# Scores of a decay attention: q and k taken as float32 products of 64 rows per head, in place of float16 halves turned by DMA

## The chip, the cores and the metric

The kernel runs on one core of a Trainium2 chip. A core has a matrix engine (TensorE: PE for its products, PEld for its weight loads), a vector engine (VectorE: DVE), a scalar engine (ScalarE: ACT), GpSimd (POOL) and SyncE (SP), which here only issues transfers. The metric is the device time of one execution in microseconds; lower is better.

## The reference

Decay attention over 8 batches of 8 heads (576 tokens, 64 numbers per head), then a two-layer block over the 4608 tokens:

```python
scores = scale * np.matmul(q, k.transpose(0, 1, 3, 2))
cum = np.cumsum(np.log(np.clip(f, 0.0001, 1.0)), axis=-1)
decay = cum[:, :, :, None] - cum[:, :, None, :]
scores = np.where(causal, -1e9, scores + decay)
attn = softmax(scores)               # rows
x = np.matmul(attn, v)               # to (4608, 512)
h = x @ w_in                         # 512 x 2048
g = np.where(h >= 1, h, np.where(h <= -1, 0, (h + 1) ** 2 / 4))
out = g @ w_out                      # 2048 x 512
```

## The kernel before

**Units of work.** Attention goes by pairs of heads. `jobs` lists 36 pairs p: batch 0 is cut in two by rows (8 jobs, p = 0 to 7), batch 1 gives p = 8 to 11, batches 2 to 7 give p = 12 to 35, four to a batch. A pair's scores are made in row blocks r = 0 to 4 of 128 rows (the last has 64, and holds both heads in the two halves of the partitions), each over the columns up to its diagonal: 128, 256, 384, 512 and 576 wide.

**How q and k are made ready** (`prepare`, lines 385 to 427; `early_prepare`, lines 362 to 383). For p under NQK = 12 the two heads lie side by side in the 128 partitions after PE has turned the blocks (line 377) and ACT has copied them out of PSUM (lines 381 and 383). The copy of q goes to two places, one per head, where the other head's 64 partitions are zero; so a head's score is one float32 product over 128 rows (line 481). From p = 12 on, q and k are scaled and split into float16 halves: ACT takes the largest size (line 395), `across` spreads it over the partitions with two small PE products (lines 120 and 130) and some DVE steps, `scale_of` makes the scales, ACT writes the high parts (lines 413 and 414), DVE the low parts and a copy (lines 415, 418, 422), and one DMA transpose on SP's queue turns all of it into `qkT` (line 425). A head's score is then two float16 products over 128 rows, high and low parts stacked (line 487).

**What follows a score block.** POOL builds the decay row (lines 491 and 495), DVE adds it to the product and takes the minimum (line 574), ACT makes the exponentials (line 578), ACT and DVE write float16 halves (lines 592 and 598), a DMA transpose turns them (lines 604 and 607), and PE multiplies by v (line 618). Of the accumulators, tile `s` has two buffers of 512 columns, one for each head of a block; tile `big` has one buffer of 1024 columns, which takes both heads of block r = 4 and the products with v.

**The two-layer block** runs in units of 256 tokens by 256 of the 2048 columns: 24 products at line 660 (48 shorter ones where the tokens straddle two batches) and 12 at line 688, with ACT and DVE between them (lines 669 to 674). The last loop of the function spreads the units that are ready over the four pairs of a batch, so some 18 units of the batch before lie between the steps of a batch's pairs, and the last units run alone at the end.

**Order.** The tile framework orders each engine's instructions by a simulated timeline of its own; each engine then runs its list in that order.

Of the kernel before, what the change touches and what calls it, by code (L numbers as in the profile page):

```python
# [8 lines left out]
F32 = mybir.dt.float32  # L9
F16 = mybir.dt.float16  # L10
# [19 lines left out]
NQK = 12  # L30
# [16 lines left out]
def kernel(  # L47
# [18 lines left out]

    nc = tc.nc
# [15 lines left out]
    ncut = NPAIR * sum(len(c) for c in CUTS.values())  # L83
# [55 lines left out]
    cq = const.tile([P, NT5, B * H], F32, name="cq")  # L139

    def decay_sums():
# [22 lines left out]
        nc.vector.tensor_copy(cq.rearrange("p t n -> p (t n)"), pt[:, 0:NT5 * nb])  # L164
# [138 lines left out]
    for t in qk32 + [v32]:  # L303
        nc.gpsimd.memset(t, 0.0)
# [6 lines left out]
    def load(ji):  # L311
# [9 lines left out]
        for j, src in enumerate((q, k)):  # L321
            s_ = src[w.b, h0:h0 + 2]
            t0 = 0 if j else w.r0
            nt = w.r1 - t0
            x = flat[:, j * 2 * NT5 * D:j * 2 * NT5 * D + 2 * nt * D]
            w.x32.append(x)
            if ji < NQK:
                dst = x.rearrange("p (t h d) -> p h t d", t=nt, h=2)
            else:
                dst = x.rearrange("p (h t d) -> p h t d", t=nt, h=2)  # L330
                if ji < max(NQK, ncut) + 2 and w.r1 == NT5:
                    nc.gpsimd.memset(dst[64:P, :, nt - 1, :], 0.0)
# [22 lines left out]
    early_qk = [two.tile([P, 3, 2, SP], F16, name="qkT") for i in range(2)]  # L355
    early_qk = [t.rearrange("p c h s -> p (c h s)").bitcast(F32)[:, 0:3 * S].rearrange("p (c s) -> p c s", c=3) for t in early_qk]
    cq8 = const.tile([P, NT5, 2 * H], F32, name="cq8")
    for t in early_qk:
        for h in range(2):
            nc.gpsimd.memset(t[64 - 64 * h:128 - 64 * h, h, :], 0.0)  # L360

    def early_prepare(w):

        if w.p == 0:
            nc.vector.tensor_scalar(out=cq8, in0=cq[:, :, 0:2 * H], scalar1=8.0, scalar2=None, op0=ALU.mult)
        t_ = early_qk[(w.p + NQK) % 2]
        w.nsig, w.nalpha = -8.0, -0.125
        bh = w.b * H + 2 * w.hp
        w.cqs = cq8[:, :, bh:bh + 2]
        w.q, w.k = t_, t_[:, 2]  # L370
        for j in range(2):
# [6 lines left out]
            if j == 0:  # L378
                for h in range(2):
                    rows = slice(64 * h, 64 * h + 64)  # L380
                    nc.scalar.activation(t_[rows, h, 0:n], pt[rows, 0:n], AF.Copy)
            else:
                nc.scalar.activation(t_[:, 2, 0:n], pt[:, 0:n], AF.Copy)

    def prepare(w):
        if w.p < NQK:
            return early_prepare(w)
        p = w.p
        bh = w.b * H + 2 * w.hp
        nq, nk = w.r1 - w.r0, w.r1  # L390
        qs = one.tile([P, 3, 2, NT5, P], F16, name="qs").rearrange("p c h t e -> p (c h t e)")
        m2 = tiny.tile([P, 2], F32, name="m2q")
        for j in range(2):
            n = w.x32[j].shape[1]
            nc.scalar.activation(qs[:, j * 2 * NT5 * D:j * 2 * NT5 * D + n], w.x32[j], AF.Abs, accum_out=m2[:, j:j + 1])  # L395
        mk = tiny.tile([P, 2], F32, name="mk")
        across(mk, m2)
        sc = tiny.tile([P, 2], F32, name="sc")
        scale_of(sc, mk, mk)
        sig = tiny.tile([P, 1], F32, name="sig")  # L400
        nc.vector.tensor_scalar(out=sig, in0=sc[:, 0:1], scalar1=sc[:, 1:2], scalar2=8.0, op0=ALU.mult, op1=ALU.mult)
        w.nsig = tiny.tile([P, 1], F32, name="nsig")
        nc.vector.tensor_scalar(out=w.nsig, in0=sig, scalar1=-1.0, scalar2=None, op0=ALU.mult)
        w.nalpha = tiny.tile([P, 1], F32, name="nalpha")
        nc.vector.reciprocal(w.nalpha, w.nsig)
        w.cqs = tiny.tile([P, NT5, 2], F32, name="cqs")
        nc.vector.tensor_scalar(out=w.cqs, in0=cq[:, :, bh:bh + 2], scalar1=sig, scalar2=None, op0=ALU.mult)

        nqe = 2 * nq * P
        qq = qs[:, 0:nqe].rearrange("p (b e) -> p b e", e=P)  # L410
        kk = qs[:, nqe:nqe + 4 * nk * P].rearrange("p (c b e) -> p c b e", c=2, e=P)
        xq, xk = (x.rearrange("p (b d) -> p b d", d=D) for x in w.x32)
        nc.scalar.activation(qq[:, :, 0:D], xq, AF.Copy, scale=sc[:, 0:1])
        nc.scalar.activation(kk[:, 0, :, 0:D], xk, AF.Copy, scale=sc[:, 1:2])
        nc.vector.scalar_tensor_tensor(
            out=qq[:, :, D:P], in0=xq, scalar=sc[:, 0:1], in1=qq[:, :, 0:D], op0=ALU.mult, op1=ALU.subtract
        )
        nc.vector.scalar_tensor_tensor(
            out=kk[:, 1, :, 0:D], in0=xk, scalar=sc[:, 1:2], in1=kk[:, 0, :, 0:D], op0=ALU.mult, op1=ALU.subtract
        )  # L420
        dup = kk.rearrange("p c b e -> p (c b) e")
        nc.vector.tensor_copy(dup[:, :, D:P], dup[:, :, 0:D])
        n = nqe + 4 * nk * P
        qkT = two.tile([P, 3, 2, SP], F16, name="qkT").rearrange("p c h s -> p (c h s)")
        nc.sync.dma_start_transpose(qkT[:, 0:n].rearrange("p (b e) -> p b e", e=P), qs[:, 0:n])
        w.q = qkT[:, 0:nqe].rearrange("p (h s) -> p h s", h=2)
        w.k = qkT[:, nqe:n].rearrange("p (c h s) -> p c h s", c=2, h=2)
# [33 lines left out]
    def scores(w, r):  # L461

        wid = min(P * (r + 1), S)
        q0 = P * r
        sds = []
        for h in range(2):
            p0, p1 = (0, P) if r < LAST else (64 * h, 64 * h + 64)
# [10 lines left out]
            for c0 in range(0, wid, 512):  # L478
                c1 = min(wid, c0 + 512)
                if w.p < NQK:  # L480
                    nc.tensor.matmul(  # L481
                        sp[p0:p1, c0:c1], lhsT=w.q[:, h, q0 - w.s0:q0 - w.s0 + p1 - p0], rhs=w.k[:, c0:c1],
                        start=True, stop=True,
                    )
                    continue
                for c in range(2):
                    nc.tensor.matmul(  # L487
                        sp[p0:p1, c0:c1], lhsT=w.q[:, h, q0 - w.s0:q0 - w.s0 + p1 - p0],
                        rhs=w.k[:, c, h, c0:c1], start=(c == 0), stop=(c == 1),
                    )  # L490
            nc.gpsimd.tensor_scalar(  # L491
                out=sd[p0:p1, 0:wid], in0=w.ck[h][p0:p1, 0:wid], scalar1=w.nsig if w.p < NQK else w.nsig[p0:p1],
# [67 lines left out]
    def weights(w, r):  # L560
# [11 lines left out]
        for i, (sd, sp) in enumerate(sds):  # L572
            a = sd[:, 0:wid]
            nc.vector.tensor_tensor_reduce(  # L574
                out=a, in0=sp[:, 0:wid], in1=a, scale=w.nalpha, scalar=BIG, op0=ALU.add, op1=ALU.min,
# [269 lines left out]
```

## Time and profile before

| | |
|---|---|
| median of 3 runs | 1206.32 us (1205.17 to 1208.73) |
| the profiled execution | 1203.55 us, of which 1201.8 us is the span of the profile |
| busy share: PE, DVE, ACT, POOL | 88%, 69%, 66%, 37% |
| products on PE | 8577 |
| share of 16 DMA engines | 62% |
| mean granted clock of PE | 0.95 |

A busy share is a mean over the whole span; its first 300 us (batches 0 and 1, and the weights' conversion), the 750 us after (batches 2 to 7) and the last 150 us (the two-layer block alone) differ, and the prediction reads them apart. In a row of the timeline the first number is the start, the second how long the row's merged instructions took from the first start to the last end; products on PE overlap each other, so the step from one row's start to the next row's start says what a row occupied.

### The profile page before, as it was taken

Reading aid. Unit: us, or ns where it says so; the run is one execution under the profiler, and the core shown is the slowest. Engines: PE = TensorE matmul, PEld = TensorE weight load, DVE = VectorE, ACT = ScalarE, POOL = GpSimd, SP = SyncE. Lnnn points to the kernel's source line nnn. Section 1 sums busy time; section 2 is a strip of 40 time slices with the busy share of each in tenths; the row PEclk is TensorE's granted clock in tenths of the full one; section 3 lists DMA queues with packets and bytes.
Section 4 is the critical chain, followed back from the end, with each engine's and each line's share of the span. In section 5 each row is a group of like instructions: output and inputs, shape, how many; then the busy total and the mean of one; then the engine's idle time right before and its main releaser. Section 6 shows DMA issues by size and latency. Waiting matters only on the chain. (4 is left out here: it accounts for less than half of the span.)

```text
span 1201.8 us, 24489 instructions
## 1 busy us (share of the span) xinstructions
PE 1063.1 (88%) x8577; PEld 696.6 (58%) x8577; DVE 834.0 (69%) x2399; ACT 796.6 (66%) x1666; POOL 450.5 (37%) x699
## 2 busy tenths in 40 slices
PE   4577678997699979998999999998899889999998
PEld 3444344564466656666666666656665566677665
DVE  6879989885777687769666868757776778522222
ACT  4675665974677687858677668857776767644443
POOL 5648634642544254425342325423542354000000
PEclk9878788998699999999999999999999989999999
DMA  8857544778887678677755848776978586300000
GB/s 239 254 174 189 130 122 97 137 142 181 160 144 158 146 164 153 147 161 158 145 121 127 155 88 173 153 148 134 169 141 180 115 155 113 73 19 2 18 19 18
DMA packets 439259, 160.05 MB, mean 133 GB/s; under 512 B 414944, under 2 KB 415968, under 8 KB 439136
## 3 DMA queue, kind: packets, MB, share of 16 engines
q1 hardware_dynamic: 439136, 158.49, 62.3%
q8 instruction: 67, 1.10, 0.4%
q14 instruction: 56, 0.46, 0.1%
HBM read 75.64 MB, written 9.58 MB: 71 GB/s over the span
## 5 line engine op out<-in xcount | busy, mean ns | idle before, releaser
L660 PE MATMUL ph<-x,place 128*128 128x256 f16 (+3 forms) x4608 | 451.2, 251 | 23.3 <-DVE u L671 15.5
L688 PE MATMUL po<-place,g 128*128 128x512 f16 x1728 | 426.3, 384 | 18.8 <-ACT g L673 12.5
L660 PEld LDWEIGHTS <-place 128*128 128x128 f16 x4608 | 368.3, 100 | 108.1 <-issue 29.4
L688 PEld LDWEIGHTS <-g 128*128 128x128 f16 x1728 | 163.8, 99 | 184.1 <-ACT g L673 17.0
L491 POOL TENSOR_SCALAR sdr<-ck,nsig,cqs 128x128 f32<-128x128 f32 (+1 forms) x192 | 163.6, 856 | 176.4 <-DVE pr L598 160.5
L578 ACT ACTIVATE sdr<-sdr,nm 128x384 f32<-128x384 f32 (+1 forms) x248 | 138.1, 557 | 73.2 <-DVE nm L574 65.8
L671 DVE SCALAR_TENSOR_TENSOR u<-ph,z,u 128x512 f32<-128x512 f32 x136 | 101.4, 746 | 108.2 <-ACT u L670 107.1
L669 ACT ACTIVATE u<-ph,z 128x512 f32<-128x512 f32 x136 | 104.5, 768 | 91.2 <-PE ph L660 91.0
L491 POOL TENSOR_SCALAR sd<-ck,nsig,cqs 64x576 f32<-64x576 f32 x48 | 46.6, 971 | 276.7 <-DMA ck<-cum_d 85.1
L673 ACT ACTIVATE g<-u,z 128x512 f16<-128x512 f32 x136 | 97.5, 718 | 78.9 <-DVE u L671 78.4
L674 DVE SCALAR_TENSOR_TENSOR g<-u,z,g 128x512 f16<-128x512 f32 x136 | 103.9, 765 | 62.1 <-ACT g L673 61.6
L598 DVE SCALAR_TENSOR_TENSOR pr<-sdr,rc,pr 128x384 f16<-128x384 f32 (+2 forms) x232 | 125.5, 570 | 27.1 <-ACT pr L592 26.3
L592 ACT ACTIVATE pr<-sdr,rc 128x384 f16<-128x384 f32 (+1 forms) x236 | 119.7, 555 | 18.0 <-issue 6.3
L574 DVE CUSTOM_DVE_ANT_0 sdr<-s,sdr,nalpha 128x128 f32<-128x128 f32 (+1 forms) x192 | 103.8, 544 | 23.0 <-POOL sdr L495 10.6
L495 POOL TENSOR_SCALAR_AFFINE_SELECT sdr<-sdr 128x128 f32<-128x128 f32 x248 | 97.3, 403 | 10.5
L487 PE MATMUL s<-qkT 128*128 128x128 f16 (+3 forms) x384 | 85.0, 310 | 17.9 <-DVE nm L574 17.3
L670 ACT ACTIVATE u<-u 128x512 f32<-128x512 f32 x144 | 89.8, 623 | 2.5
L487 PEld LDWEIGHTS <-qkT 128*128 128x128 f16 (+1 forms) x576 | 46.6, 103 | 58.1 <-issue 35.0
L618 PE MATMUL big<-pT,vs 128*64 128x320 f16 (+3 forms) x1098 | 72.4, 284 | 2.0 <-DVE nm L574 2.0
L395 ACT ACTIVATE qs<-qk 128x640 f16<-128x640 f32 x48 | 34.9, 729 | 52.8 <-DMA qkT<-qs 44.9
L618 PEld LDWEIGHTS <-vs 128*64 128x64 f16 x1098 | 49.4, 112 | 30.2 <-issue 8.0
L481 PE MATMUL s<-qkT 128*128 128x128 f32 (+3 forms) x128 | 53.5, 520 | 10.6 <-DVE nm L574 8.8
(169 smaller groups left out, 1170.8 us busy)
## 6 DMA issues: line engine op xcount, KB each, us to landing
ck<-cum_d SPq DMA_DIRECT2D x64, 288.0 KB, 3.8
out_dram<-ot SPq DMA_DIRECT2D x36, 256.0 KB, 2.5
qk<-in_k_dram SPq DMA_DIRECT2D x64, 128.0 KB, 2.9
ck<-in_v_dram SPq DMA_DIRECT2D x28, 288.0 KB, 3.1
v<-in_v_dram SPq DMA_DIRECT2D x62, 128.0 KB, 2.8
qk<-in_q_dram SPq DMA_DIRECT2D x56, 128.0 KB, 2.6
place<-in_moe_w_in_dram SPq DMA_DIRECT2D x12, 512.0 KB, 5.4
place<-in_moe_w_out_dram SPq DMA_DIRECT2D x10, 512.0 KB, 6.6
```

What stands on the lines that cost most here:

```text
L487: nc.tensor.matmul(sp[p0:p1, c0:c1], lhsT=w.q[:, h, q0 - w.s0:q0 - w.s0 + p1 - p0], rhs=w.k[:, c, h, c0:c1], start=(c == 0), stop=(c == 1),)
L491: nc.gpsimd.tensor_scalar(out=sd[p0:p1, 0:wid], in0=w.ck[h][p0:p1, 0:wid], scalar1=w.nsig if w.p < NQK else w.nsig[p0:p1], scalar2=w.cqs[p ...
L574: nc.vector.tensor_tensor_reduce(out=a, in0=sp[:, 0:wid], in1=a, scale=w.nalpha, scalar=BIG, op0=ALU.add, op1=ALU.min, accum_out=nm[:, i:i ...
L578: nc.scalar.activation(a, a, AF.Exp, bias=nm[:, i:i + 1], scale=-1.0, accum_out=sm[:, i:i + 1])
L592: nc.scalar.activation(pr[:, :, 0, i, :], a, AF.Copy, scale=rc[:, i:i + 1])
L598: nc.vector.scalar_tensor_tensor(out=pr[:, :, 1, i, :], in0=a, scalar=rc[:, i:i + 1], in1=pr[:, :, 0, i, :], op0=ALU.mult, op1=ALU.subtract,)
L618: nc.tensor.matmul(av[64 * h:64 * h + 64, at + s0:at + s1], lhsT=w.vs[:, vl, h, t, :], rhs=w.pT[:, t, pl, h, s0:s1], start=(t == 0 and pi ...
L660: nc.tensor.matmul(ph[:, fi, a0:a1], lhsT=wi[fb][:, wl, t, fi * P:(fi + 1) * P], rhs=xs[b][:, t, xl, s0:s0 + a1 - a0], start=(fi == 0 and ...
L669: nc.scalar.activation(u, h, AF.Relu, scale=z.u[:, i:i + 1], bias=z.h[:, i:i + 1])
L671: nc.vector.scalar_tensor_tensor(out=u, in0=h, scalar=z.t[:, i:i + 1], in1=u, op0=ALU.max, op1=ALU.min)
L674: nc.vector.scalar_tensor_tensor(out=g[:, 1], in0=u, scalar=z.r[:, i:i + 1], in1=g[:, 0], op0=ALU.mult, op1=ALU.subtract)
L688: nc.tensor.matmul(po[ch][i], lhsT=g[:, gl, fi * TC + i * P:fi * TC + (i + 1) * P], rhs=wo[fb][:, wl, fi, :], start=(first and fi == 0 and ...
```

## The change

`prepare` becomes one function for all 36 pairs: PE turns q and k blocks in float32 (line 362 after the change), ACT copies q once and k once, the two heads lying in partitions 0 to 63 and 64 to 127. A head's score is one float32 product over its own 64 partitions (line 417); the zeros beside q are gone, and so are, for p from 12 on, the largest sizes, scales, halves and the DMA transpose. The scales become the constants -8 and -0.125. In a score block the products of the two heads are written next to each other in the program.

```diff
     def prepare(w):
-        if w.p < NQK:
-            return early_prepare(w)
...
-            nc.scalar.activation(qs[:, j * 2 * NT5 * D:j * 2 * NT5 * D + n], w.x32[j], AF.Abs, accum_out=m2[:, j:j + 1])
-        across(mk, m2)
-        scale_of(sc, mk, mk)
...
-        nc.scalar.activation(qq[:, :, 0:D], xq, AF.Copy, scale=sc[:, 0:1])
-        nc.scalar.activation(kk[:, 0, :, 0:D], xk, AF.Copy, scale=sc[:, 1:2])
-        nc.vector.scalar_tensor_tensor(
-            out=qq[:, :, D:P], in0=xq, scalar=sc[:, 0:1], in1=qq[:, :, 0:D], op0=ALU.mult, op1=ALU.subtract
-        )
...
-        nc.vector.tensor_copy(dup[:, :, D:P], dup[:, :, 0:D])
-        nc.sync.dma_start_transpose(qkT[:, 0:n].rearrange("p (b e) -> p b e", e=P), qs[:, 0:n])
+        t_ = two.tile([P, 2, S], F32, name="qkT")
+        w.cqs = cq8[:, :, bh:bh + 2]
+        w.q, w.k = t_[:, 0], t_[:, 1]
+        for j in range(2):
+            pt = ps1.tile([P, 1024], F32, name="big")
+            t0 = 0 if j else w.r0
+            n = w.s1 - P * t0
+            for c0 in range(0, n, P):
+                m = min(P, n - c0)
+                nc.tensor.transpose(pt[:, c0:c0 + m], w.x32[j][0:m, c0:c0 + P], ident[0:m, 0:m])
+            nc.scalar.activation(t_[:, j, 0:n], pt[:, 0:n], AF.Copy)
...
     def scores(w, r):
-                for c in range(2):
-                    nc.tensor.matmul(
-                        sp[p0:p1, c0:c1], lhsT=w.q[:, h, q0 - w.s0:q0 - w.s0 + p1 - p0],
-                        rhs=w.k[:, c, h, c0:c1], start=(c == 0), stop=(c == 1),
-                    )
+        for c0 in range(0, wid, 512):
+            c1 = min(wid, c0 + 512)
+            for h, (p0, p1) in enumerate(rows):
+                nc.tensor.matmul(
+                    sds[h % len(sds)][1][p0:p1, c0:c1],
+                    lhsT=w.q[64 * h:64 * h + 64, q0 - w.s0:q0 - w.s0 + p1 - p0],
+                    rhs=w.k[64 * h:64 * h + 64, c0:c1], start=True, stop=True,
+                )
```

PE's list before, at a score block 256 columns wide of a pair past 12: the two float16 products of one head, a product of the two-layer block, then those of the other head.

```order
L487 LDWEIGHTS qkT
L487 MATMUL s<-qkT 128x256
L487 LDWEIGHTS qkT
L487 MATMUL s<-qkT 128x256
L688 LDWEIGHTS g
L688 MATMUL po_9811<-place_97,g 128x512
L487 LDWEIGHTS qkT
L487 MATMUL s<-qkT 128x256
L487 LDWEIGHTS qkT
L487 MATMUL s<-qkT 128x256
```

PE's list after, at blocks r = 3 (`s`, 512 wide) and r = 4 (`big`, 64 rows per head) of such a pair; L417 is a float32 product of 64 rows, L621 and L593 are the two-layer block's.

```order
L417 MATMUL big<-qkT 64x512 x2
L417 MATMUL s<-qkT 128x512
L621 LDWEIGHTS g
L621 MATMUL po_11910<-place_91,g 128x512
L621 LDWEIGHTS g
L621 MATMUL po_11910<-place_91,g 128x512
L621 LDWEIGHTS g
L621 MATMUL po_11911<-place_91,g 128x512
L621 LDWEIGHTS g
L621 MATMUL po_11911<-place_91,g 128x512
L417 MATMUL s<-qkT 128x512
L417 MATMUL big<-qkT 64x64 x2
```

A head has one product where it had two; the two heads of block r = 3 stand apart here, with products of 128 rows between them, while those of block r = 4 stand together. Over the 24 pairs from p = 12 on, the list after has 192 such products for r = 0 to 3, in 142 separate places; 41 times the two heads of a block stand side by side (15 of 128 columns, 13 of 256, 8 of 384, 5 of 512).

PE's list after, where a pair's q is turned (L362) ahead of the first score block of the pair before it:

```order
L362 MATMUL big<-ident,qk_1_115 128x128 x4
L362 MATMUL big<-ident,qk_1_115 128x64
L417 MATMUL s<-qkT 128x128 x2
L621 LDWEIGHTS g
L621 MATMUL po_10998<-place_95,g 128x512
```

These five turns, and five more for k, were not on PE for p from 12 on. Two stretches of SP's list, before and after, where a pair's q and k are fetched (qk), its decay row (ck) and the values:

```order
L607 DMA_TRANSPOSE pT<-pr_6372 128x10x64 x2
L442 DMA v_116<-in_v_dram 128x4x64 x2
L444 DMA v_116<-in_v_dram 64x2x64
L708 DMA out_dram<-ot 128x512 x2
L335 DMA qk_0_114<-in_q_dram 128x4x64 x2
L339 DMA qk_0_114<-in_q_dram 64x2x64
L425 DMA_TRANSPOSE qkT<-qs 128x30x128
L346 DMA ck<-cum_d 128x576
```

```order
L540 DMA_TRANSPOSE pT<-pr_6130 128x10x64 x2
L378 DMA v_116<-in_v_dram 128x4x64 x2
L380 DMA v_116<-in_v_dram 64x2x64
L330 DMA qk_0_114<-in_q_dram 128x4x64 x2
L334 DMA qk_0_114<-in_q_dram 64x2x64
L330 DMA qk_0_114<-in_k_dram 128x4x64 x2
L334 DMA qk_0_114<-in_k_dram 64x2x64
L641 DMA out_dram<-ot 128x512 x2
L341 DMA ck<-cum_d 128x576
```

The transpose of 30 blocks is gone from SP's list; the fetches around it stay.

More of the change, by code (lines that the diff above doesn't have):

```diff
@@ L29 @@
 NPE = 5
-NQK = 12
 POOL_LOW = {6: (2, 4), 7: (2, 4)}
@@ L163, in decay_sums @@
             )
-        nc.vector.tensor_copy(cq.rearrange("p t n -> p (t n)"), pt[:, 0:NT5 * nb])
+        nc.vector.tensor_scalar(
+            out=cq8.rearrange("p t n -> p (t n)"), in0=pt[:, 0:NT5 * nb], scalar1=8.0, scalar2=None, op0=ALU.mult
+        )
     place = [const.tile([P, 2, 2 * DM], F16, name=f"place{i}") for i in range(2 * NB + 1)]
@@ L302 @@
     sd4 = [const.tile([P, SP], F32, name=f"sd4_{i}") for i in range(2)]
-    for t in qk32 + [v32]:
-        nc.gpsimd.memset(t, 0.0)
+    nc.gpsimd.memset(v32, 0.0)
     for t in sd4:
@@ L326, in load @@
             w.x32.append(x)
[L327 to L332, printed above, removed]
+            dst = x.rearrange("p (t h d) -> p h t d", t=nt, h=2)
             full = min(w.r1, LAST)
@@ L354, with prepare @@
     prs = [one.tile([P, PRN[r]], F16, name=f"pr{r}").bitcast(F32) for r in range(NT5)]
[L355 to L367, printed above, removed]
+    def prepare(w):
+        t_ = two.tile([P, 2, S], F32, name="qkT")
         bh = w.b * H + 2 * w.hp
         w.cqs = cq8[:, :, bh:bh + 2]
-        w.q, w.k = t_, t_[:, 2]
+        w.q, w.k = t_[:, 0], t_[:, 1]
         for j in range(2):
@@ L477, in scores @@
                 sds.append((sd, sp))
[L478 to L485, printed above, removed]
-                for c in range(2):
-                    nc.tensor.matmul(
-                        sp[p0:p1, c0:c1], lhsT=w.q[:, h, q0 - w.s0:q0 - w.s0 + p1 - p0],
-                        rhs=w.k[:, c, h, c0:c1], start=(c == 0), stop=(c == 1),
-                    )
+        for c0 in range(0, wid, 512):
[5 more added lines that the diff above has]
+                    rhs=w.k[64 * h:64 * h + 64, c0:c1], start=True, stop=True,
+                )
+        for h, (p0, p1) in enumerate(rows):
+            sd = sds[h % len(sds)][0]
             nc.gpsimd.tensor_scalar(
-                out=sd[p0:p1, 0:wid], in0=w.ck[h][p0:p1, 0:wid], scalar1=w.nsig if w.p < NQK else w.nsig[p0:p1],
+                out=sd[p0:p1, 0:wid], in0=w.ck[h][p0:p1, 0:wid], scalar1=-8.0,
                 scalar2=w.cqs[p0:p1, r, h:h + 1], op0=ALU.mult, op1=ALU.add,
```

42 lines of the change are left out of this document (3 added, 39 removed).

## The prediction

> **What bounds the kernel now.** I read the busy time by stage first, then the chain of waits, then PE's timeline where it is dense. By stage (columns: stretch, its length, then busy us of PE, PEld, DVE, ACT, POOL with instruction counts, granted clock, DMA share, GB/s):
>
> ```profile
> 0.00:300.00 300.00, 221.69 (x1316) 135.44 (x1317) 241.55 (x745) 190.49 (x425) 158.51 (x232) 0.88 0.67 167
> 300.00:1050.00 750.00, 693.99 (x6049) 460.33 (x6049) 549.83 (x1601) 542.49 (x1151) 291.97 (x468) 0.97 0.73 144
> 1050.00:1201.00 151.00, 147.46 (x1214) 100.79 (x1212) 42.60 (x57) 63.64 (x91) 0.00 (x0) 1.00 0.04 15
> ```
>
> In the first 300 us PE idles 78 us and DVE is the busiest (242). In the 750 us that hold the pairs from p = 12 on, PE is busy 694 and idle 56, DVE and ACT near 73%: PE is the bound. Is a busy PE a full PE? The chain of waits, where the two-layer block runs alone:
>
> ```profile
> 1077.13 2.59 PE po L688 x12
> 1079.72 2.68 PE ph L660 x48
> ```
>
> Twelve products of 512 columns in 2.59 us are 216 ns each, one column per 0.42 ns, without a pause. The middle stage shows the same step (0.43 for two such products, from 874.32 to 874.75 below), so its PE has 56 us to give and no more. Its waits are few (columns: who waited for whom, us, times, longest):
>
> ```profile
> PE s L487 <- DVE nm L574: 16.7, 14, 5.2
> PE ph L660 <- DVE u L671: 12.9, 7, 3.4
> PE po L688 <- ACT g L673: 8.8, 7, 2.8
> ...
> PEld L487 <- issue: 33.3, 58, 5.6
> ```
>
> The last row is the weight load from `qkT`; "issue" means the profile shows nothing that it waited for, and the DMA transpose that writes `qkT` is what is left.
>
> **What leaves PE, per pair from p = 12.** A row's price is the step to the next row's start. PE's timeline at such a pair:
>
> ```profile
> 860.70 0.27 PE L120 MATMUL s<-ident,m2q 128*2 128x128 f32 x1
> 860.81 0.28 PE L487 MATMUL s<-qkT 128*128 128x128 f16 x2
> 860.92 1.84 PE L660 MATMUL ph<-x,place 128*128 128x64 f16 x30
> ...
> 866.04 0.38 PE L130 MATMUL s<-dg,ones 2*128 2x2 f32 x2
> 866.35 0.93 PE L660 MATMUL ph<-x,place 128*128 128x192 f16 x13
> ...
> 868.84 0.38 PE L487 MATMUL s<-qkT 128*128 128x256 f16 x2
> 869.06 0.59 PE L688 MATMUL po<-place,g 128*128 128x512 f16 x2
> ...
> 872.26 0.49 PE L487 MATMUL s<-qkT 128*128 128x384 f16 x2
> 872.58 1.06 PE L660 MATMUL ph<-x,place 128*128 128x64 f16 x16
> 873.57 0.69 PE L487 MATMUL big<-qkT 128*64 128x512 f16 x8
> 874.19 0.29 PE L660 MATMUL ph<-x,place 128*128 128x64 f16 x2
> 874.32 0.59 PE L487 MATMUL s<-qkT 128*128 128x512 f16 x2
> 874.75 0.28 PE L660 MATMUL ph<-x,place 128*128 128x64 f16 x2
> ```
>
> One head takes 0.11, 0.22, 0.32 and 0.43 us for its blocks r = 0 to 3 (two products each): 1.08, two heads 2.16. Block r = 4 takes 0.62, line 130 takes 0.31, line 120 takes 0.11, and two entries into a smaller shape take some 0.09 each (shown below). That is 3.38 us; times 24 pairs, **81 us leave PE**.
>
> **What comes to PE.** The pairs under p = 12 have float32 products already, and turned q and k:
>
> ```profile
> 41.51 0.86 PE L377 MATMUL big<-ident,qk 128*128 128x128 f32 x5
> 42.29 0.27 PE L120 MATMUL s<-ident,m 128*1 128x128 f32 x1
> ...
> 263.75 0.60 PE L660 MATMUL ph<-x,place 128*128 128x256 f16 x4
> 264.27 1.20 PE L481 MATMUL big<-qkT 128*64 128x512 f32 x8
> 265.41 0.72 PE L660 MATMUL ph<-x,place 128*128 128x256 f16 x5
> 265.96 0.81 PE L481 MATMUL s<-qkT 128*128 128x384 f32 x2
> 266.61 0.93 PE L660 MATMUL ph<-x,place 128*128 128x256 f16 x7
> 267.38 1.02 PE L481 MATMUL s<-qkT 128*128 128x512 f32 x2
> 268.24 0.71 PE L660 MATMUL ph<-x,place 128*128 128x256 f16 x5
> ```
>
> - *Products, r = 0 to 3.* A float32 product (two records, x2) of 384 columns takes 0.65, of 512 columns 0.86: twice the float16 pair. I give 64 rows the price of 128, as it is the columns that stream. By columns a head costs 0.22 + 0.43 + 0.65 + 0.86 = 2.16, two heads 4.3, 24 pairs 104 us.
> - *Heads that overlap.* Where both heads stand side by side, do they run at once? For halves of the output columns they do: block r = 4 in float32 has two heads of 576 columns, alone 0.97 each (0.86 x 576 / 512), and took 1.14 with entry and exit. For halves of the rows no row of this trace shows it; the ends are nothing and a whole head saved. By the count in the order (15 of 128, 13 of 256, 8 of 384, 5 of 512) that is 15 x 0.22 + 13 x 0.43 + 8 x 0.65 + 5 x 0.86 = 18 us. I take 18, by the nearest row, the one of block r = 4.
> - *Block r = 4.* 1.14 by the row above, 24 times 27; eleven of the 24 stand in pieces in the order, so 30.
> - *Entering and leaving the row halves.* From 263.75 four products of 0.109 end at 264.18, and the next starts at 264.27: 0.09 to enter. Five turns from 41.51 take 0.78; four full ones at a quarter of a 512-column record (0.107) and one half make 0.48, so entering and leaving the 64-row shape took 0.30. The 142 places are then 24 us (0.17, what block r = 4 paid: 1.14 less 0.97) to 43; I take 0.25, 36 us.
> - *Turning q and k.* 2 x 0.78 a pair, 37 us; a few share their entry with a product beside them, so 35.
>
> Together 104 - 18 + 30 + 36 + 35 = 187, less 81: **PE gains 106 us of work** in a stage in which it idles 56.
>
> The Trainium skill ("TensorE: Matmul & The Clock Gate", Part 3) says that products in different row groups run at once, some 4 ns apart; by it the 18 us are saved, without it the sum is 124. The Trainium skill ("TensorEngine Tiling (Array Packing)", Gotcha 1: PSUM Pressure) says that different row tiles cannot use one bank of PSUM at the same time. Both heads of block r = 4 write one buffer of `big`; by that page they would run one after the other, and the sum would be 19 us higher (24 x 0.8).
>
> **What leaves the other engines.** The rows (mean ns of one before the bar's end):
>
> ```profile
> L395 ACT ACTIVATE qs<-qk 128x640 f16<-128x640 f32 x48 | 34.9, 729 | 52.8 <-DMA qkT<-qs 44.9 <-issue 6.8 <-DMA qk<-in_q_dram 1.1
> L413 ACT ACTIVATE qs<-qk,sc 128x640 f16<-128x640 f32 x24 | 19.7, 820 | 3.3 <-DVE sc L110 3.1
> L383 ACT ACTIVATE qkT<-big 128x576 f32<-128x576 f32 x8 | 5.2, 645 | 2.0 <-PE big L377 1.9
> L415 DVE SCALAR_TENSOR_TENSOR qs<-qk,sc,qs 128x640 f16<-128x640 f32 x24 | 23.7, 987 | 2.9 <-ACT qs L413 2.6
> L425 SPq DMA_TRANSPOSE qkT<-qs x24: 4500/4730/5660, 269.6 to 998.3; - x24
> ```
>
> Per pair ACT loses two passes of 0.73 and two of 0.82 (line 414 like 413) and gains two copies of 0.645: 1.8 us less. DVE loses two splits of about 1.0 and more small steps, over 2 us; SP's queue loses a transpose of 4.7 us. None of these is the bound, so this pays only through PE's 56 us of waiting. Gone with certainty is the wait on the transpose; waits on DVE and ACT shrink, since both do less while PE takes longer over a pair. Ends: nothing and 56 us back; I take 30. What is late next: the copies out of `big`, in the rivals. In the first 300 us the lone float32 heads pay the same visits, some 15 us of PE against 78 of idle, and one ACT copy a pair goes; DVE's weight conversion, untouched, leads there. I count 0, ends -10 and +15.
>
> **Sum.** 106 - 30 = 76 us more than the profiled execution's 1203.55, which lies 2.8 under the median of 1206.32: 1280 against 1204, or **1282** against the median.
>
> **The rivals.**
> - *The row halves do not overlap.* Then 18 us come back, and with block r = 4 one after the other 19 more: 1319. For it: no row shows row halves at work. Against: the column halves overlap in float16 and float32.
> - *`big` becomes the wait.* It has one buffer, and per pair two more uses, each held until ACT has copied. The turns of the early pairs waited:
>
> ```profile
> L377 PE MATMUL big<-ident,qk 128*128 128x128 f32 x72 | 15.8, 339 | 15.0 <-issue 3.9 <-DVE x L628 3.5 <-ACT qkT L381 3.4
> ```
>
>   15 us over 12 jobs, 1.25 a job, 24 pairs: +30, so 1312. Against: the order puts products of the two-layer block between most turns and what needs them.
> - *Faster: the added work falls into PE's gaps.* If entering and leaving cost nothing between two products (-36), the added work is 70 us, 2.9 a pair. If all 56 us of waiting go, and the granted clock of the middle stage rises from 0.97 to 1 (0.03 x 694 = 21), that makes 70 - 77 = -7: 1199. It decides where the added work falls under 3.2 us a pair (77 / 24); I count 4.4. Against it stand the 0.09 and the 0.30, read in this trace.
>
> **How the numbers follow.** Forecast 0.62, no overlap 0.18, `big` 0.13, gaps 0.07. What this kernel's measurement can tell from no change is about 0.3%, 4 us. The gaps' case splits into 0.05 faster and 0.02 the same; the rest is slower, 0.93. The low end keeps most of the 56 us as given back and visits at 0.17 (1282 - 26 - 11 = 1245, and 5 for the early stage); the high end takes in both other slower cases (1319, 1312) and an idle time that gives back little. Range 1240 to 1340.
>
> **What would show it.** In the profile after: PE busy in the middle stage above 95% and the tail as before; lone products of line 417 at 0.43 us per record of 512 columns, and where heads stand side by side, a step of some 0.9 us for two heads (1.7 would mean no overlap); gaps of 0.1 to 0.2 us on both sides of a lone head; ACT and DVE less busy; no wait on a transpose of q and k. The forecast is wrong if 64-row products stream faster than 128-row ones, or if PE's idle time in the middle stage does not shrink.

## The result and the profile after

The changed kernel took **1238.31 us** (median of 4 runs, 1237.71 to 1241.65) against 1205.81 for the kernel before (4 runs): ratio **1.027**, 95% interval 1.0245 to 1.0295. It is slower, as forecast, but by 32.5 us where 76 were forecast; 1238 lies 2 us under the low end of the range. The profiled execution took 1237.71, of which 1235.7 is the span. One run of the kernel before, among those measured later, took 2146.17 us; no ratio below counts it.

First the busy time by stage of the profile after, with the columns as before:

```profile
0.00:300.00 300.00, 238.40 (x1332) 134.32 (x1332) 237.08 (x736) 183.31 (x413) 154.25 (x222) 0.86 0.66 162
300.00:1050.00 750.00, 743.42 (x5970) 454.66 (x5971) 453.11 (x1229) 499.29 (x1016) 224.43 (x459) 0.99 0.53 111
1050.00:1235.00 185.00, 181.05 (x1445) 120.55 (x1443) 59.98 (x98) 83.91 (x131) 3.82 (x8) 1.00 0.10 25
```

In the middle stage PE idles 7 us of 750 where it idled 56. DVE fell by 97 us, ACT by 43, POOL by 68, the DMA share from 0.73 to 0.53, and the granted clock rose from 0.97 to 0.99. The stage after 1050 us is longer by 34: what PE did not get done among the pairs is done at the end. PE's waits between 300 and 1085 us show the same thing; the three that led before (16.7, 12.9 and 8.8 us) are now:

```profile
PE s L417 <- DVE nm L507: 3.8, 4, 2.0
PE ph L593 <- DVE u L604: 1.4, 1, 1.4
...
PE po L621 <- ACT g L606: 0.4, 1, 0.4
```

PE's timeline after shows what a product of half the rows occupies (start, duration, shapes; a price is the step to the next start):

```profile
701.80 0.91 PE L417 MATMUL s<-qkT 64*128 64x384 f32 x2
702.64 0.72 PE L593 MATMUL ph<-x,place 128*128 128x256 f16 x5
...
707.17 1.12 PE L417 MATMUL s<-qkT 64*128 64x512 f32 x2
708.23 1.90 PE L621 MATMUL po<-place,g 128*128 128x512 f16 x8
...
714.70 1.18 PE L417 MATMUL big<-qkT 64*64 64x512 f32 x6
715.82 1.90 PE L621 MATMUL po<-place,g 128*128 128x512 f16 x8
...
739.48 0.80 PE L362 MATMUL big<-ident,qk 128*128 128x128 f32 x5
740.02 0.75 PE L417 MATMUL s<-qkT 64*128 64x256 f32 x4
...
744.38 0.92 PE L417 MATMUL s<-qkT 64*128 64x384 f32 x4
745.22 2.03 PE L593 MATMUL ph<-x,place 128*128 128x256 f16 x17
```

One head of 384 columns alone takes 0.84 us (701.80 to 702.64). Two of them side by side take 0.84 as well (744.38 to 745.22, x4). A lone head of 512 columns takes 1.06, where its two records stream for 0.86.

Because busy times have modelled ends, I also counted PE's time from the starts of consecutive products, from 300 us to the end: a product's columns at 0.417 ns (0.834 in float32) is streaming; extra steps at a change to or from a smaller shape are "shape"; the extra step between the two records of a 64-row float32 product is "load" (about 0.1 us); the few ns between any two products are "small"; the excess while the granted clock is under 1 is "clock"; the rest is "wait". The count begins with the first product that starts after 300 us, so a wait across that moment is left out: 8.1 us in e10_passes_again, 4.0 in e11_all_again, 3.9 in e1_full_rows, 2.0 in the changed kernel, 1.0 or less in the others. The sorting is mine and good to some us (all in us):

| kernel | streaming | shape | load | small | clock | wait | total |
|---|---|---|---|---|---|---|---|
| before | 773.3 | 21.7 | 0 | 18.3 | 14.6 | 69.6 | 897.5 |
| after | 837.3 | 43.3 | 13.9 | 18.7 | 6.3 | 10.4 | 929.8 |
| e1_full_rows | 850.7 | 24.6 | 0 | 20.2 | 4.1 | 16.9 | 916.5 |
| e2_one_s_tile | 815.4 | 38.9 | 9.5 | 18.2 | 4.2 | 33.7 | 919.8 |
| e3_twice_before | 850.0 | 24.3 | 0 | 20.4 | 3.7 | 28.3 | 926.6 |
| e5_late_one_tile | 806.8 | 36.9 | 9.3 | 19.1 | 4.3 | 28.7 | 905.1 |
| e7_twice_after | 942.0 | 40.3 | 13.1 | 21.0 | 4.9 | 11.8 | 1033.1 |
| e8_early_halves | 775.3 | 21.7 | 0 | 18.7 | 15.2 | 73.3 | 904.2 |
| e9_transposes_again | 843.6 | 45.8 | 16.4 | 19.8 | 4.9 | 29.7 | 960.1 |
| e10_passes_again | 835.1 | 42.5 | 13.4 | 18.7 | 4.2 | 8.5 | 922.4 |
| e11_all_again | 836.8 | 43.7 | 13.5 | 18.8 | 8.3 | 18.9 | 940.1 |
| e12_late_one_full_turns | 806.8 | 31.9 | 11.2 | 17.6 | 8.3 | 22.5 | 898.4 |

So PE gained 64.0 + 21.6 + 13.9 = **99.5 us of work** (forecast: 106), and got back 59.2 of waits and 8.3 of slow clock, **67.5 us** (forecast: 30). The difference, 32, is the result. The first 300 us bring no difference: by their end PE has started 614 products into `ph` and `po` in either kernel. The open question is why so much came back.

The row of weight loads at the lone head of 512 columns tells where "load" arises:

```profile
707.17 0.29 PEld L417 LDWEIGHTS s<-qkT 64*128 64x128 f32 x2 [0.42 <-issue]
```

Both loads have ended by 707.46, and the second record starts at 707.70: it does not wait for its own weights. What is late is the first record's load, which starts only as that record does; the step to the second record is 0.53 there. The 128-row float32 products of e1_full_rows show the same rule at 512 columns: where the first record's load begins 0.11 us or more ahead of it the step is 0.43, at 0.08 ahead it is 0.46, at 0.05 it is 0.49, and 0.53 where it begins with the record.

### The profile page after: what moved, and what is told of

Same layout as the page of the kernel before. It is cut to its first block, busy times and chain, and to the rows that moved or that the text cites. A ratio compares the mean times of both kernels' runs of the same rounds, so it can differ in the third digit from the quotient of the medians.

```text
span 1235.7 us, 24329 instructions
## 1 busy us (share of the span) xinstructions
PE 1162.9 (94%) x8745; PEld 709.5 (57%) x8745; DVE 750.2 (61%) x2062; ACT 766.5 (62%) x1558; POOL 382.5 (31%) x689
## 5 line engine op out<-in xcount | busy, mean ns | idle before, releaser
L593 PE MATMUL ph<-x,place 128*128 128x256 f16 (+3 forms) x4608 | 437.3, 249 | 7.8 <-POOL place L226 3.9
L593 PEld LDWEIGHTS <-place 128*128 128x128 f16 x4608 | 353.8, 99 | 115.8 <-issue 54.0
L621 PE MATMUL po<-place,g 128*128 128x512 f16 x1728 | 415.7, 382 | 4.1 <-ACT g L606 3.4
L424 POOL TENSOR_SCALAR sdr<-ck,cq 128x384 f32<-128x384 f32 (+1 forms) x248 | 162.4, 655 | 465.1 <-DVE pr L531 398.5
L621 PEld LDWEIGHTS <-g 128*128 128x128 f16 x1728 | 162.4, 98 | 188.7 <-issue 18.2
L417 PE MATMUL s<-qkT 64*128 64x512 f32 (+3 forms) x512 | 181.0, 520 | 11.2 <-DVE nm L507 9.6
L602 ACT ACTIVATE u<-ph,z 128x512 f32<-128x512 f32 x136 | 104.7, 770 | 115.2 <-PE ph L593 114.6
L507 DVE CUSTOM_DVE_ANT_0 sdr<-s,sdr 128x384 f32<-128x384 f32 (+1 forms) x248 | 119.5, 491 | 70.4 <-PE s L417 53.0
L417 PEld LDWEIGHTS s<-qkT 64*128 64x128 f32 x512 | 66.4, 204 | 62.3 <-DVE nm L507 23.2
L424 POOL TENSOR_SCALAR sd<-ck,cq 64x576 f32<-64x576 f32 x64 | 52.0, 813 | 152.3 <-DMA ck<-cum_d 104.5
L428 POOL TENSOR_SCALAR_AFFINE_SELECT sdr<-sdr 128x128 f32<-128x128 f32 x248 | 89.7, 372 | 13.4
L362 PE MATMUL big<-ident,qk 128*128 128x128 f32 (+1 forms) x328 | 61.3, 295 | 11.7 <-DVE x L561 3.5
L363 ACT ACTIVATE qkT<-big 128x576 f32<-128x576 f32 (+2 forms) x72 | 43.5, 604 | 32.4 <-PE big L362 31.5
```

The source lines that it names most:

```text
L417: nc.tensor.matmul(sds[h % len(sds)][1][p0:p1, c0:c1], lhsT=w.q[64 * h:64 * h + 64, q0 - w.s0:q0 - w.s0 + p1 - p0], rhs=w.k[64 * h:64 * h ...
L424: nc.gpsimd.tensor_scalar(out=sd[p0:p1, 0:wid], in0=w.ck[h][p0:p1, 0:wid], scalar1=-8.0, scalar2=w.cqs[p0:p1, r, h:h + 1], op0=ALU.mult, o ...
L507: nc.vector.tensor_tensor_reduce(out=a, in0=sp[:, 0:wid], in1=a, scale=-0.125, scalar=BIG, op0=ALU.add, op1=ALU.min, accum_out=nm[:, i:i + 1],
L593: nc.tensor.matmul(ph[:, fi, a0:a1], lhsT=wi[fb][:, wl, t, fi * P:(fi + 1) * P], rhs=xs[b][:, t, xl, s0:s0 + a1 - a0], start=(fi == 0 and ...
L602: nc.scalar.activation(u, h, AF.Relu, scale=z.u[:, i:i + 1], bias=z.h[:, i:i + 1])
L621: nc.tensor.matmul(po[ch][i], lhsT=g[:, gl, fi * TC + i * P:fi * TC + (i + 1) * P], rhs=wo[fb][:, wl, fi, :], start=(first and fi == 0 and ...
```

## The experiments

Three theories. **Length**: PE waits less because its own list got longer, so that the steps of DVE and ACT that it waits for are done in time; then work added to PE alone gives the waits back too. **Relief**: PE waits less because DVE and ACT lost the passes over q and k; then putting those back brings the waits back. **Transfers**: it is the lost DMA transposes. A second set of runs asks for the price of the row halves. The kernel before was measured beside each set of runs, at 1205.81 to 1209.30 us, so a difference of 3 us or so between runs of different sets says nothing.

### Only more work on PE

The kernel before, each float16 product from p = 12 on issued twice, the second pass writing over the first; DVE, ACT and the transfers are as they were:

```diff
-                for c in range(2):
+                for c in (0, 1, 0, 1):
```

> The kernel before with each float16 score product of pairs 12 to 35 issued twice (the second time over the first, same values), nothing else: PE gets 64 us of work (24 x 2.7), all other engines, scales and DMA transposes stay. If longer PE work by itself hides PE's waits (70 us of them in the middle stage before, 22 after the change), the time is 1215 to 1230, as the waits shrink by 40 to 50 us. If the waits went because the q and k chain (ACT, DVE, DMA transpose) went, they stay here: 1262 to 1275.

Measured: 1232.93 us, ratio 1.0204 (1.0177 to 1.0230): 25.6 over the 1207.37 of the kernel before beside it. That is 3 us above the numbers that length gave, and 29 us below those of its rival. Its middle stage and PE's leading wait there:

```profile
300.00:1050.00 750.00, 732.37 (x6400) 481.71 (x6398) 543.66 (x1575) 531.76 (x1120) 280.33 (x464) 0.99 0.72 141
```

```profile
PE s L487 <- DVE nm L574: 7.5, 6, 4.9
```

DVE and ACT are as busy as in the kernel before, and the transposes are all there (DMA share 0.72). Yet the wait on DVE fell from 16.7 to 7.5 us, all waits from 69.6 to 28.3, and the slow clock's share from 14.6 to 3.7. The added 76.7 us of streaming (64 were expected) cost 25.6. A longer list on PE is enough to bring back some 50 us. One thing comes with it, in this run as in every other: the framework orders the lists anew, and in PE's some score products stand dozens of two-layer products earlier or later than before. No run separates the length of PE's list from the order that goes with it.

Nor was a wait on the DMA transpose of q and k among what the change took away. Of the transposes of the kernel before, the trace says who waited for them:

```profile
L425 SPq DMA_TRANSPOSE qkT<-qs x24: 4500/4730/5660, 269.6 to 998.3; - x24
...
who waited for it (us, times):
  ACT qs L395: 44.9, 20
```

ACT waited to write `qs` again; PE did not wait. Each of the 24 had landed 2.7 to 24 us before the first product that reads it.

### The same on the changed kernel

Each score product of the changed kernel from p = 12 on is written twice to the same place:

```diff
+                for again in range(2 if w.p >= 12 else 1):
...
+                        lhsT=w.q[64 * h:64 * h + 64, q0 - w.s0:q0 - w.s0 + p1 - p0],
+                        rhs=w.k[64 * h:64 * h + 64, c0:c1], start=True, stop=True,
```

> The changed kernel with every score product of pairs 12 to 35 issued twice (the second over the first). Its late stage has 22 us of PE waits left, so if PE is full nearly all of the added product time shows: 75 to 110 us more, 1313 to 1348. If the added time still falls into waits at the rate of the doubled kernel before (26 of 77 us), 30 to 40 us more, 1268 to 1278.

Measured: 1341.33 us, ratio 1.1093 (1.1071 to 1.1116), 103 over the changed kernel, within the numbers of a full PE. Streaming grew by 104.7 us, and the waits stayed (10.4 and 11.8). With the waits gone every added microsecond shows; the same sort of work cost a third of its length on the kernel before.

### The passes of ACT and DVE put back

The changed kernel with stand-ins for what it lost: per pair from p = 12 on two largest-size passes and two copies on ACT, two splits, a copy and ten small steps on DVE. Nothing reads their results. In the first version they read q and k as these arrive (and zeros are written over the buffers of q and k once at the start):

```diff
+        if w.p >= 12:
+            for j in range(2):
+                nc.scalar.activation(spare[:, j * n:(j + 1) * n], w.x32[j], AF.Abs, accum_out=m2[:, j:j + 1])
...
+                nc.vector.scalar_tensor_tensor(
+                    out=spare[:, (j + 2) * n:(j + 3) * n], in0=w.x32[j], scalar=0.5, in1=spare[:, j * n:(j + 1) * n],
...
+            nc.vector.tensor_copy(spare[:, 4 * n:6 * n], spare[:, 0:2 * n])
```

> The changed kernel with the removed ACT and DVE passes put back as idle work for pairs 12 to 35 (two Abs passes with sums and two copies on ACT, two splits, a copy and ten small steps on DVE, into a spare tile that nothing reads), and zeros written over the q and k buffers once at the start. PE's list has the same products. If the relief of ACT and DVE is what took PE's waits away, they come back: 1265 to 1290. If not, 1236 to 1248.

Measured: 1254.86 us, ratio 1.0411 (1.0364 to 1.0458), 16.5 over the changed kernel, between the two numbers expected. It does not tell what it was meant to tell, since a wait came with it, as ACT's waits show:

```profile
ACT qs L370 <- DMA qk<-in_q_dram: 51.0, 20, 4.1
```

ACT stood 51 us for the transfer of q with its other work queued behind. The next version reads the turned q and k in place of `w.x32`, which are in SBUF by then:

```diff
+            parts = (flat[:, 0:n], flat[:, 2 * S - n:2 * S])
...
+                nc.scalar.activation(spare[:, j * n:(j + 1) * n], parts[j], AF.Abs, accum_out=m2[:, j:j + 1])
```

> The changed kernel with the removed ACT and DVE passes put back as idle work, now on the turned q and k, so that ACT does not stand waiting for a transfer (it stood 48 us in the first try). If the relief of ACT and DVE is worth much to PE, 1250 to 1260 as in the first try; if longer PE work hides them, 1236 to 1246.

Measured: 1234.60 us, ratio 1.0226 (1.0203 to 1.0249): 3.7 below the changed kernel. The middle stage:

```profile
300.00:1050.00 750.00, 738.67 (x5988) 456.37 (x5990) 524.50 (x1531) 548.58 (x1154) 244.90 (x460) 0.99 0.54 112
```

DVE has 71 us of its 97 again and ACT all of its 43, and no time is lost. The waits are 8.5 us by the table, and with the one across 300 us, which its leading row of waits shows as the longest, 16.6, where the changed kernel has 12.4:

```profile
PE s L435 <- DVE nm L525: 10.1, 4, 8.1
```

So the passes bring back some 4 us of 59, and relief falls as the main cause.

### The transposes put back

A DMA transpose of 28 blocks per pair from a spare tile, released by a step that follows the arrival of q. First by DVE:

```diff
+        if w.p >= 12:
+            nc.vector.tensor_copy(spare[0:64, 0:1], w.x32[0][0:64, 0:1])
+            turned = one.tile([P, 28, P], F16, name="turned")
+            nc.sync.dma_start_transpose(turned, spare)
```

> The changed kernel with a DMA transpose of 28 blocks per pair from 12 on put back on SP's queue, from and to spare tiles that nothing reads (and one small DVE copy ahead of each). PE waits for none of them. If the load on the DMA engines and on SP's queue held PE up before, the time rises by 10 to 25 us; if only PE's wait for the turned q and k did, it stays within 4 us of 1238.

Measured: 1269.99 us, ratio 1.0501 (1.0468 to 1.0533): 31.7 over the changed kernel, more than either number expected. Like the first run of the passes it carries a wait of its own, here on DVE:

```profile
DVE spare L367 <- DMA qk<-in_q_dram: 60.4, 23, 5.5
```

So the release was moved behind the copy out of `big` on ACT:

```diff
+            nc.scalar.activation(spare[:, 0:1], pt[:, 0:1], AF.Copy)
+            turned = one.tile([P, 28, P], F16, name="turned")
+            nc.sync.dma_start_transpose(turned, spare)
```

> The changed kernel with the spare DMA transpose per pair once more, but released by a one-column ACT copy behind the turned k instead of a DVE copy that waited for a transfer (in the first try DVE stood 56 us for it). If the load on DMA and SP's queue itself holds PE up, 1250 to 1275 again. If the rise of the first try was DVE standing still, 1236 to 1246.

Measured: 1265.87 us, ratio 1.0493 (1.0461 to 1.0524): still 27.6 over the changed kernel, though DVE's wait is gone. Taken alone this speaks for transfers; but by the table only 19.3 of the 30 us that PE's time grew by are waits, and 11 are PE's own work (6.3 streaming, 2.5 shape, 2.5 load), in a list ordered anew. The last run puts passes and transposes back together, the transpose reading what the passes wrote, as in the kernel before:

```diff
             nc.vector.tensor_copy(spare[:, 4 * n:6 * n], spare[:, 0:2 * n])
+            turned = one.tile([P, 28, P], F16, name="turned")
+            nc.sync.dma_start_transpose(turned, spare[:, 0:28 * P])
```

> The changed kernel with both put back: the ACT and DVE passes of the run before, and behind them the spare DMA transpose. What the other engines and the DMA did before is then there again, and only PE's own list and its wait for the transpose differ. If PE's longer list is what hides the waits, PE waits 25 to 40 us in the late stage and the time is 1240 to 1258. If the waits went because work left the other engines, they are back at some 70 us: 1280 to 1295.

Measured: 1246.95 us, ratio 1.0326 (1.0303 to 1.0349), 8.6 over the changed kernel and within the time expected of a longer list, with fewer waits than the 25 to 40 us expected there. Its middle stage:

```profile
300.00:1050.00 750.00, 736.96 (x5879) 451.04 (x5880) 526.32 (x1558) 543.20 (x1147) 253.03 (x460) 0.98 0.69 139
```

DVE, ACT and the DMA share are near what they were before the change (POOL, with no stand-in, has 253 us of its 292), and PE waits 18.9 us instead of 10.4, or 22.9 instead of 12.4 with the waits across 300 us. So of the 59 us of waits that went, some 8 to 11 went because the other engines and queues were relieved, and about 50 are gone with that work back in place. The stand-ins stand later in a pair's chain than the real passes did, and no product waits for them; but the kernel with doubled products kept the real ones where they were, and lost 41 us of waits all the same.

The same transposes cost 28 us alone and 12 on top of the passes (1246.95 against 1234.60). Of the 20 us that lie between PE's times in the two runs with transposes, 10.8 are waits and 12 PE's own work (6.8 streaming, 2.1 shape, 2.9 load), less 3.4 of clock; why the waits differ stays open. SP's waits ahead of the transposes do not explain it: they add up to 101.5 us where the transposes cost 28, and to 142.6 where they cost 12. POOL's wait for the decay rows, which SP fetches, goes the right way. POOL's waits with the transposes alone, and with everything back:

```profile
POOL sd L430 <- DMA ck<-cum_d: 150.6, 30, 13.8
```

```profile
POOL sd L444 <- DMA ck<-cum_d: 92.1, 24, 13.1
```

The changed kernel has 104.5 there. That would fit an order of SP's list in which the transposes hold up the fetches, but no run moved that order alone.

### Float32 without the row halves

The kernel before, with the way of its early pairs (float32, turned by PE, zeros in the other head's rows, 128 rows) taken for all 36:

```diff
-NQK = 12
+NQK = 36
...
-    cq8 = const.tile([P, NT5, 2 * H], F32, name="cq8")
+    cq8 = const.tile([P, NT5, B * H], F32, name="cq8")
```

> All 36 pairs take q and k in float32, but as the kernel before does it for its first 12 pairs: products over 128 rows with zeros beside q, no row halves. If PE's own work sets the middle stage, the row halves are worth what they cost and save on PE: without them 18 us of overlap go (late pairs) and some 24 to 36 us of entering and leaving go too, one more half copy of q per pair goes to ACT (0.64 us). That gives 1222 to 1234. If the row halves pay in all, 1242 or more. If PE's work is not what sets the time, 1238.

Measured: 1225.61 us, ratio 1.0146 (1.0118 to 1.0173). Without row halves float32 costs 18 us over the kernel before, and the changed kernel 13 us more than that. By the table the halves save 13.4 us of streaming where heads overlap, and cost 18.7 in changes of shape and 13.9 in loads. They cost more than they save, as the two heads seldom stand together; 6.5 us less of waits give a part of it back.

The counterpart for the early pairs alone, the kernel before with row halves for p under 12:

```diff
-        w.q, w.k = t_, t_[:, 2]
+        w.q, w.k = t_[:, 0], t_[:, 2]
...
-                        sp[p0:p1, c0:c1], lhsT=w.q[:, h, q0 - w.s0:q0 - w.s0 + p1 - p0], rhs=w.k[:, c0:c1],
-                        start=True, stop=True,
+                        sp[p0:p1, c0:c1], lhsT=w.q[64 * h:64 * h + 64, q0 - w.s0:q0 - w.s0 + p1 - p0],
+                        rhs=w.k[64 * h:64 * h + 64, c0:c1], start=True, stop=True,
```

> The kernel before with the row halves in its first 12 pairs alone: one copy of q, no zeros, products over 64 rows; pairs from 12 on as before. If the early stage is not set by PE, 1203 to 1210, the same as before. If entering and leaving the row halves counts there as well, 1212 to 1225.

Measured: 1206.30 us, ratio 0.9971 (0.9942 to 1.0000): by its interval between 0.6% less and no change. The early part of the change is worth about what the forecast gave it, 0.

### The two heads brought together

In the changed kernel each head of a block has its own buffer of `s`. With one buffer for both, they become free together, and stand together:

```diff
-                    sp = ps.tile([P, 512], F32, name="s")
+                    if h == 0:
+                        both = ps.tile([P, 2, 512], F32, name="s", bufs=1)
+                    sp = both[:, h]
```

> The changed kernel with both heads' accumulators in one tile of 1024 columns, so that both heads' products become ready together and stand side by side in PE's order (nearly all blocks, against 41 of 96 in the late pairs). Theory that PE's work sets the time: some 30 us of products overlap in the late pairs and about 20 us of entering and leaving go, 1185 to 1200. Rival that the later release counts (a block waits until DVE has read both heads of the block before, 0.75 us more in 96 blocks): the gain is eaten, 1225 to 1260.

Measured: 1227.18 us, ratio 1.0167 (1.0135 to 1.0199). A miss for the theory, and within the numbers of the rival: 11 us won where more than 38 were expected. PE's timeline shows that the heads do stand together:

```profile
712.80 1.13 PE L419 MATMUL s<-qkT 64*128 64x512 f32 x4
713.86 2.36 PE L595 MATMUL ph<-x,place 128*128 128x256 f16 x20
```

Two heads of 512 columns in 1.06 us, what one took alone. The loss is in the early stage:

```profile
0.00:300.00 300.00, 211.33 (x1228) 124.18 (x1230) 222.24 (x687) 173.79 (x392) 135.61 (x218) 0.84 0.62 154
```

1228 products by 300 us where the changed kernel has 1332. There the pairs run almost by themselves; the likely reason is that with one buffer the next block's products wait until both heads of this one are read. So the buffers were kept apart until p = 12 and joined from there on:

```diff
+        if p == 12:
+            own.close()
+            sbox[:] = [own.enter_context(tc.tile_pool(name="ps_both", bufs=1, space=bass.MemoryType.PSUM)), True]
...
-                    sp = ps.tile([P, 512], F32, name="s")
+                    if not sbox[1]:
+                        sp = sbox[0].tile([P, 512], F32, name="s")
+                    else:
+                        if h == 0:
+                            both = sbox[0].tile([P, 2, 512], F32, name="s")
+                        sp = both[:, h]
```

> The changed kernel with two score tiles for pairs 0 to 11 as it has them, and one tile of 1024 columns for both heads from pair 12 on. The run with one tile throughout lost some 20 us to PE's waits in the first 300 us and did 22 us less of the two-layer block there. If that is where its gain went, this kernel comes to 1200 to 1212, level with the kernel before. If the late pairs' longer waits for the one tile (20 us more there) grow as well, 1215 to 1230.

Measured: 1211.86 us against 1209.30, ratio 1.0013 (0.9990 to 1.0036). Of the 41.5 us of PE's work that went against the changed kernel (30.5 streaming, 6.4 shape, 4.6 load), 18.3 came back as waits. That is what length gives in the other direction, but the one tile also comes free later than two, and this run does not tell the two apart.

The last run adds one thing. The last block of q and k has 64 tokens, and its turn is a 64-row product; here it is turned as a full block, with zeros or old values below, whose columns are not copied:

```diff
-                m = min(P, n - c0)
-                nc.tensor.transpose(pt[:, c0:c0 + m], w.x32[j][0:m, c0:c0 + P], ident[0:m, 0:m])
+                nc.tensor.transpose(pt[:, c0:c0 + P], w.x32[j][:, c0:c0 + P], ident)
```

> One tile for both heads from pair 12 on, and the last block of q and k turned as a full block of 128 rows (the lower 64 hold zeros or old values, and their columns are not copied), so that turning never enters the 64-row shape. Some 45 turns in the late pairs lose 0.25 us of entering and leaving and gain 0.05: 5 to 9 us less than the 1212 of the version without, 1202 to 1207. If entering and leaving is hidden there, 1210 to 1214.

Measured: **1204.78 us** (12 runs, 1197.76 to 1211.27) against 1208.86, ratio **0.9965** (0.9946 to 0.9985), within the expected numbers. By the table 5.0 us of shape went against the version without, as meant; loads took 1.9 us more, waits fell by 6.2 and the slow clock took 4.0 more, which was not forecast. It is the one version that beats both kernels with 1 outside its interval, by a third of a per cent over the kernel before. PE's timeline:

```profile
724.00 0.71 PE L366 MATMUL big<-ident,qk 128*128 128x128 f32 x5
724.64 0.70 PE L426 MATMUL s<-qkT 64*128 64x256 f32 x4
...
729.28 0.92 PE L426 MATMUL s<-qkT 64*128 64x384 f32 x4
730.13 1.70 PE L602 MATMUL ph<-x,place 128*128 128x256 f16 x14
```

## Why the prediction was wrong

- **What PE gains was right.** Forecast 106 us of work, counted 99.5. Two parts of it moved against each other. A visit to the row halves costs more than the 0.25 taken: a lone head of 512 columns takes 1.06 to the next start and 0.09 before it, so 1.15 less 0.86, 0.29; about 0.1 of it lies between its two records, which the forecast did not have. Together the table's shape and load grew by 35.5 us, where the forecast had 36 for the visits. The turns cost less than 0.78: where a score product follows, five take 0.54 (739.48 to 740.02), as the shape is left once for both.
- **The overlap of the row halves holds**, and its rival (1319) falls: 0.84 us for two heads of 384 columns and for one, and in the trace the two heads' records start 6 to 7 ns apart. The Trainium skill ("TensorE: Matmul & The Clock Gate", Part 3) agrees with this row. Over the run the overlap saved 13.4 us of streaming against e1_full_rows, where the forecast had 18. The heads of block r = 4, which share one buffer of `big`, ran at once too: 1.12 us (714.70 to 715.82) for 576 columns of one head and 512 of the other, where one after the other would be 1.83. The rule of the Trainium skill ("TensorEngine Tiling (Array Packing)", Gotcha 1: PSUM Pressure) did not make them serial here; the measurement decides.
- **`big` did not become the wait** (rival 1312). The page after has, for the turns of all 36 pairs, less idle time ahead (11.7 us) than the 15.0 us that the turns of 12 jobs had before:

```profile
L362 PE MATMUL big<-ident,qk 128*128 128x128 f32 (+1 forms) x328 | 61.3, 295 | 11.7 <-DVE x L561 3.5
```

- **The step that failed is the term "given back"**: "Ends: nothing and 56 us back; I take 30". It was 59 us of waits and 8 of slow clock. Its bound was wrong first: the 56 us were the idle time of a row whose busy times have modelled ends, and by the starts of the products the waits were 69.6 from 300 us on, with 14.6 more lost to a granted clock under 1. The page's own row already shows more than 30: idle 56 before, 7 after. The clock was left out of the forecast's sum, and stood only in the rival that ends faster. Nor was "the wait on the transpose", which the forecast took as gone with certainty, ever a wait of PE: the row that it read so (PEld L487 <- issue, 33.3 us) is idle time of the weight loads that the profile puts down to nothing (the doubled kernel, whose waits are gone by 41 us, still has 30.9 there), and every transpose had landed before PE came to it.
- **Its reason failed with it.** The forecast let the waits shrink "since both do less while PE takes longer over a pair" and gave the relief equal weight. The runs put 8 to 11 of the 59 us down to relief (everything back: waits 10.4 to 18.9), and 41 us of waits go with a longer list and the order that comes with it, and nothing relieved (doubled products: 69.6 to 28.3). The rest, some 10 us, no run assigns: the changed list is longer still (99.5 us against 76.7), and POOL's relief was not put back. My reading, not shown by itself: a pair's chain through DVE and ACT has a length of its own, and what PE does meanwhile is nearly free until PE's list is as long as the chain. Of the rivals, the one in which the work falls into the gaps had the room right: its 77 us (56 of idle, 21 of clock) in place of the 30 make the forecast's own sum 106 - 77 = 29, or 1235, against 1238.31 measured. That the total came so close is in part luck, as the clock gave 8 and the waits 59. Its other condition, visits at no cost, did not hold.
- **The early stage** was counted at 0, and is: 614 products into `ph` and `po` by 300 us in both kernels, and next to no change from the early row halves alone.
- **What would show it** came out in the main: PE busy 99% of the middle stage, DVE and ACT less busy, two heads in the time of one. A lone record of 512 columns takes 0.53, not 0.43, and the stage after 1050 us did not stay as before. No wait on a transpose of q and k is there, but there was none before.

## What to carry to other kernels

Idle time of an engine that is "the bound" at 93% is room that added work on that same engine can fill: here 77 us of products cost 26, and once the waits were gone the next 105 cost 103. So count the waits from the starts of instructions, and expect added work to take most of them. When an engine's work is cut, expect some of it to come back as waits (41 us less work, 18 us of waits back, though the one tile may have its part in that). Row halves paid here only where the two halves stood side by side in the engine's list, and what put them there was the buffer that both write: one tile for both heads in the stage that has other work to run, two where it has none.

## What the runs showed of the hardware

- A float32 product's first record stretches by as much as its own weight load lacks of a lead of 0.11 us (steps of 0.43, 0.46, 0.49 and 0.53 us at leads of 0.11, 0.08, 0.05 and 0). A lone product of 64 rows between 128-row ones has no lead and pays 0.1 us; with 0.09 to enter and about as much to leave, a lone head costs some 0.3 us beyond its columns. Between 300 us and the end shape and load grew by 35.5 us.
- Two 64-row float32 products in different row halves took as long as one (0.84 and 0.84 us), and two heads that write one buffer in different partitions ran at once too (1.12 us).
- Less was lost to a slow granted clock where PE waited less: 14.6 us before the change, 3.7 to 8.3 in every version with a longer list. It is not in proportion: 33.7 us of waits go with 4.2 (e2_one_s_tile), 18.9 with 8.3 (e11_all_again).
- 24 transposes more on SP's queue cost 28 us alone and 12 on top of the passes of ACT and DVE; part of the difference is PE's list, the rest is open.
